# Row buffers kept for all batches, 24 or 25 scatter marks a batch, and later folds on VectorE

## The chip, the core and the metric

The kernel runs on one core of a Trainium2 chip. The metric is the device time of one execution in microseconds (us). The engines are TensorE (PE; its weight loads are shown as PEld), VectorE (DVE), ScalarE (ACT), GpSimd (POOL) and SyncE (SP, which here only issues DMA transfers). Each works through its own instructions in order and waits on semaphores for the others.

## The reference, cut to what matters

```python
def reference(x, moe..., moe2...):
    X = np.fft.fft(x, axis=1)              # x: 8 x 3072 x 256
    X = np.fft.fft(X, axis=2).real
    t = X.reshape(24576, 256)
    # group stage: each token goes to one of 8 experts
    logits = norm(t) @ norm(expert_emb).T / tau
    e = argmax(logits); gate = softmax(logits)[e]
    t = gate * (relu(t @ w1[e]) @ w2[e])   # 256 -> 1024 -> 256
    # gated stage, the same weights for all tokens
    return ((t @ w_a) * (t @ w_b)) @ w_out # 256 -> 1536 -> 256
```

The change lies in the first part: the two transforms, the choice of the expert, and the scatter of each token's row to its expert's region in DRAM.

## The kernel before

The transforms run over 8 batches b of 3072 points of time. The input of a batch comes in four chunks of 96x8x256 (`load_x`, three buffers). `fold_u` and `fold_v` make sums and differences of mirrored columns; a chunk has two halves of each, 96x508 elements. Folds of batch b+1 are made during batch b: `folds` puts them into queues, and `drain` takes some out at fixed places of the loops. In the kernel before, the `fold_v` of chunks 0 and 1 are whole (96x1016) and go to GpSimd through `fold_q`; all others go to VectorE through `dve_q`. Behind the folds of a chunk stands `rest`, which copies two columns on ScalarE and issues the load of the chunk three later.

A batch has two phases. **s1** has 16 groups of four matmuls (line 356), each copied to yt by ScalarE (360). **s2** has 12 steps t: two pairs of matmuls into psb and psa (377), the copy zs of psb on ScalarE (378), and zc from both on VectorE (382, two instructions). **s3** follows two steps behind s2: matmuls (395, 398) and on ScalarE the copy qs (406), and then VectorE writes two rows of tokens into xo (407, 409), 24 rows of 128 tokens a batch. The s3 steps 10 and 11 stand in the next batch, behind its first two s1 groups. `post` queues ScalarE's mirrored copies (421) and squares (416) of xo.

`route` chooses the experts of a batch: a chain of some 35 small VectorE instructions, advanced one at a time between the others, five groups of seven in s1 and the rest in s2 of the next batch. Its last one (557) makes the row positions, and only then are 24 scatters put into `pool_q`. They are indirect DMAs issued by GpSimd (164), one for each row of 128 tokens. `mark` takes one out of the queue (two when over 24 wait) behind certain ScalarE copies, and the scatter waits for that copy, so that the scatters are spread. In the kernel before, the marks are all 16 copies of s1 (of batches from 2 on) and the 12 of s2.

There are two xo buffers, for even and odd batches. In the kernel before, each batch takes a new tile from its pool; a new tile's first write waits until every use of the old tile in that memory is over. The odd buffer is also the setup's scratch space (`spare`).

In the last batch the group stage is prepared: `weigh` (756, 757) and `turn` of the first group of tokens stand in s2 at steps 6 and 8. When the transforms are over, their right-hand pools are freed, and the remaining scatters of batch 6 are issued without marks. The group stage splits its expert weights into two parts with a ScalarE cast (746) and a VectorE subtraction (747); one of these tiles lies where the even xo buffer was. After the group stage comes the gated stage, by far the longest part.

The named places of the order are these: step t means the t-th turn of the s2 loop, a turn the time from a batch's first zs copy to the next batch's.

Of the kernel before, what the change touches and what calls it, by code (L numbers as in the profile page):

```python
# [8 lines left out]
F32 = mybir.dt.float32  # L9
# [14 lines left out]
NT = 12  # L24
SEG = 67
ROW = 4 * SEG - 1
# [111 lines left out]
def moe_kernel(ctx, tc, x, emb, tau, w1, w2, wa, wb, wo, pa, pt, pr, nat, out):  # L138
    nc = tc.nc
    ve, sc, gp, pe, sy = nc.vector, nc.scalar, nc.gpsimd, nc.tensor, nc.sync  # L140
# [37 lines left out]
    def mark(i):  # L178

        marks[:] = [i.ins]  # L180
        drain(pool_q, 2 if len(pool_q) > 24 else 1)

    def scatter(idx_ap, src):
        i = spread(idx_ap, src, xs, NROWS - 1, "xs")
        if marks:
# [11 lines left out]
    xo_p = [p1b.enter_context(tc.tile_pool(name="xo0", bufs=1, side="right")),  # L197
            p1.enter_context(tc.tile_pool(name="xo1", bufs=1, side="left"))]
# [26 lines left out]
    def bank():  # L225
        uses[0] += 1
        return banks[uses[0] % 2][:, 0:384]

    def corner():
        uses[1] += 1  # L230
        return banks[uses[1] % 2][:, 384:512]
# [4 lines left out]
    def load_x(n):  # L236
        b, c = divmod(n, 4)
        if b == B:
            return
        t = xr_p.tile([96, 8, D], F32, name="xr")  # L240
        sy.dma_start(t, x[b].rearrange("(p n) d -> p n d", p=96)[:, 8 * c:8 * c + 8, :])
        xr[b, c] = t

    def pair(b, c):
        if (b, c) not in xf:
            xf[b, c] = big[(4 * b + c) % 6][0:96, :].rearrange("p (n d) -> p n d", n=8)
        return xr[b, c], xf[b, c]

    def fold_u(b, c, h):
        a, f = pair(b, c)  # L250
        n = slice(4 * h, 4 * h + 4)
        ve.tensor_tensor(f[:, n, 1:128], a[:, n, 1:128], a[:, n, 255:128:-1], ALU.add)

    def fold_v(b, c, eng, h):
        a, f = pair(b, c)
        n = slice(4 * h, 4 * h + 4) if h is not None else slice(0, 8)
        eng.tensor_tensor(f[:, n, 129:256], a[:, n, 1:128], a[:, n, 255:128:-1], ALU.subtract)

    def fold_e(b, c):
        a, f = xr.pop((b, c)), xf[b, c]  # L260
        sc.copy(f[:, :, 0:256:128], a[:, :, 0:256:128])
# [18 lines left out]
        return y  # L280


    spare = xo_p[1].tile([128, 2 * NT, ROW + 1], F32, name="xo").rearrange("p j c -> p (j c)")
    pcs = spare[:, 0:640]
    embt = spare[0:8, 640:896]
    su = ExitStack()
# [9 lines left out]
    ps = corner()  # L296
# [48 lines left out]
    xo = {}  # L345
    ssq = {}

    def s1(b, s):
        f = xf[b, s // 2]
        state["step"] += 1  # L350
        if s == 0:
            yts[b] = [yt_p.tile([128, NQ, 128], F32, name=f"yt{h}") for h in range(2)]
        for h in range(2):
            ps = bank()
            for n in range(4):
                pe.matmul(ps[:, 96 * n:96 * n + 96], lhsT=f[:, 4 * (s % 2) + n, 128 * h:128 * h + 128],
                          rhs=f1[0:96, :], start=True, stop=True)
            dst = yts[b][h][:, :, 16 * s:16 * s + 16].rearrange("p q (n c) -> p q n c", c=4)
            src = ps.rearrange("p (n q c) -> p q n c", n=4, c=4)
            i = sc.copy(dst, src)  # L360
            if b > 1:
                mark(i)
            elif b:
                marks[:] = [i.ins]
            if b:
                drain(act_q, 1)
# [19 lines left out]
    def s3(b, t):  # L386
        za, zb = zt.pop((b, t))
        if t == 0:
            xo[b] = xo_p[b % 2].tile([128, 2 * NT, ROW + 1], F32, name="xo")
            ssq[b] = r_p.tile([128, 2, NT], F32, name="ss", bufs=2)  # L390
        o = xo[b]
        ps = ps3.tile([128, 3, 137], F32, name="ps3")
        for i in range(2):
            q = 2 * t + i
            pe.matmul(ps[64 * i:64 * i + 64, 1, :], lhsT=tq(q), rhs=zb[:, i, :], start=True, stop=True)
        for i in range(2):
            q = 2 * t + i
            pe.matmul(ps[64 * i:64 * i + 64, 0, :], lhsT=tp(q), rhs=za[:, i, :], start=True, stop=True)
        pi = 0
        if t == 11:  # L400
            pi = 2
            for i in range(2):
                pe.matmul(ps[64 * i:64 * i + 64, 2, :], lhsT=tp2 if i else tp(22), rhs=za[:, i, :],
                          start=True, stop=True)
        qs = z_p.tile([128, 137], F32, name="qs")
        sc.copy(qs, ps[:, 1, :])
        ve.tensor_tensor(o[:, t, MAIN:MAIN + NCOL], ps[:, 0, :], qs, ALU.subtract)
        advance()
        ve.tensor_tensor(o[:, NT + t, MAIN:MAIN + NCOL], ps[:, pi, :], qs, ALU.add)
        advance()  # L410
# [15 lines left out]
        if t1 == NT:  # L426
            act_q.append(lambda: square(b, 1, 11))

    act_q, dve_q, pool_q, fold_q, routes = [], [], [], [], []

    def drain(q, n):
        for _ in range(min(n, len(q))):
            q.pop(0)()

    def folds(b):
        for c in range(4):
            dve_q.append(lambda c=c: fold_u(b, c, 0))
            dve_q.append(lambda c=c: fold_u(b, c, 1))
            if c < 2:
                fold_q.append(lambda c=c: fold_v(b, c, gp, None))  # L440
            else:
                dve_q.append(lambda c=c: fold_v(b, c, ve, 0))
                dve_q.append(lambda c=c: fold_v(b, c, ve, 1))

            def rest(c=c):
                fold_e(b, c)
                load_x(4 * b + c + 3)

            dve_q.append(lambda c=c, rest=rest: act_q.insert(0, rest))

    seg = {}
    for n in sorted({2 * (t1 - t0) for c in CHUNKS.values() for t0, t1 in c} | {2 * NT}):
        s = c1.tile([128, E, n], F32, name=f"seg{n}")
# [114 lines left out]
    def advance(n=1):  # L568
        for _ in range(n):
            if routes:  # L570
                for g in list(routes):
                    r = next(g, 0)
                    if r == 0:
                        routes.remove(g)
                    if r != 1:
                        break

    def start_route(b, t0, t1):
        routes.append(route(b, t0, t1, state["next"]))
        state["next"] += 1  # L580
# [368 lines left out]
    def first(c):  # L949
        for h in range(2):  # L950
            fold_u(0, c, h)
        fold_v(0, c, gp if c != 2 else ve, None)

    for b in range(B):
        last = b == B - 1
        if not last:
            folds(b + 1)
        for s in range(8):
            if b == 0 and s < 6:
                if s == 0:  # L960
                    routes.append(embed())
                if s % 2 == 0:
                    first(s // 2 + 1)
                else:
                    fold_e(0, s // 2 + 1)
                    load_x(s // 2 + 4)
            s1(b, s)
            if b or s > 5:
                drain(fold_q, 1)
            if b == 0:  # L970
                advance(7)
                drain(dve_q, s > 3)
                continue
            if s == 0:
                s3(b - 1, 10)
                s3(b - 1, 11)
                post(b - 1, 9, 12)
                act_q.append(lambda b=b - 1, c=CHUNKS.get(b - 1, ((0, NT),))[-1]: start_route(b, *c))
            if last:
                drain(act_q, s < 3)  # L980
                advance(8)
                if s == 0:
                    assert "tab1" in half
                    load_w(0)
                if s == 4:
                    load_w(1)
                if s in (4, 5):
                    split_w(0, s - 4)
            elif s < 3:
                drain(dve_q, 3 if s else 2)  # L990
                drain(act_q, s)
            else:
                advance(7)
        if b == 0:
            while routes:
                advance()
            su.close()
        chunks = {t1 + 1: (t0, t1) for t0, t1 in CHUNKS.get(b, ())}
        if last:
            for g in range(2):  # L1000
                load_g(g)
        for t in range(NT + (2 if last else 0)):
            if t < NT:
                s2(b, t)
            if t >= 2:
                s3(b, t - 2)
            if t in (5, 8, 11):
                post(b, t - 5, t - 2)
            if t == NT + 1:
                break  # L1010
            if t - 1 in chunks:
                act_q.append(lambda b=b, c=chunks[t - 1]: start_route(b, *c))
            if t % 3:
                drain(dve_q, 1)
            drain(act_q, 2)
            if last:
                advance(1)
                if t == 6:
                    weigh(0)
                if t == 8:  # L1020
                    turn(0)
        drain(dve_q, 20)
# [236 lines left out]
    for st in range(NST):  # L1259
        G, p = divmod(st, NP)  # L1260
# [60 lines left out]
```

## Time and profile before

| | |
|---|---|
| median of 3 runs | 3882.5 us (3882.05 to 3883.97) |
| profiled execution, its own time | 3879.51 us |
| its span, first to last instruction | 3877.7 us |
| mean granted TensorE clock | 0.985 of full |
| TensorE busy | 3773.7 us (97%) |
| VectorE busy | 3121.0 us (80%) |
| ScalarE busy | 1702.1 us (44%) |
| GpSimd busy | 1136.6 us (29%) |
| transforms, to the first group-stage matmul | about 381 us of the span |

Busy shares are means over stages with different limits. The change touches the first tenth of the program, so the rows below come from that stretch, with times counted from the start of the span. A row's bracket tells how long the engine was idle ahead of it and what released it.

### The profile page before, as it was taken

The page shows a single profiled execution, that of the slowest core. Times are in us where ns is not written, and L with a number is a line of the kernel's source. Part 1 is how long each engine was busy: PE and PEld are TensorE (multiplying, and loading weights), DVE is VectorE, ACT ScalarE, POOL GpSimd, SP SyncE. Part 2 cuts the span into 40 slices and gives each one's busy share as a digit, 9 for nine tenths or more (in the row PEclk, how much of TensorE's full clock was granted, in tenths as well). Part 3 has the DMA queues.
Part 4 walks back from the last instruction along what each step waited for, and adds up shares of the span by engine and source line. Part 5 has one row for each costly group of instructions (what it writes and reads, how often), then busy time and mean ns, then how long its engine had stood idle before and what let it go on. Part 6 is the DMA issues. An engine that isn't in the chain of part 4 may idle for free.

```text
span 3877.7 us, 68085 instructions
## 1 busy us (share of the span) xinstructions
PE 3773.7 (97%) x25556; PEld 3445.0 (89%) x25556; DVE 3121.0 (80%) x5097; ACT 1702.1 (44%) x3025; POOL 1136.6 (29%) x1017
## 2 busy tenths in 40 slices
PE   9888899999999999999999999999999999999998
PEld 8777899999999999888888888888888888888887
DVE  6766889899989987777788877788777788777886
ACT  4555566666666666433333333333333333333332
POOL 2666566667676643000000000000000000011011
PEclk8889899999999999999999999999999999999999
DMA  5444354333243231334334434444344344344331
GB/s 147 137 136 147 109 169 139 119 120 116 80 122 118 74 98 51 123 136 142 139 136 144 138 137 145 147 138 144 136 139 143 136 141 141 136 141 145 137 134 56
DMA packets 255048, 497.84 MB, mean 128 GB/s; under 512 B 151541, under 2 KB 184061, under 8 KB 245885
## 3 DMA queue, kind: packets, MB, share of 16 engines
q1 hardware_dynamic: 236284, 442.04, 35.1%
q0 software_dynamic: 18432, 51.44, 3.7%
q8 instruction: 201, 3.29, 0.3%
q14 instruction: 131, 1.07, 0.1%
HBM read 568.14 MB, written 95.14 MB: 171 GB/s over the span
## 4 chain that ended last, share of the span: by engine, by line
PE 59%; issue 18%; DVE 11%; POOL 2%; ACT 1%; DMA 0%; SPq 0%; POOLq 0%; ACTq 0%; DVEq 0%
PE pp L1142 7%; PE pp L1144 6%; PE pp L1143 6%; PE psy L819 5%; PE psy L820 5%; PE psy L821 5%; PE psh L794 5%; PE psh L790 5%; PE psh L792 4%; PE po L1212 3%; PE po L1210 3%; PE po L1211 3%; DVE big L1183 2%; DVE big L1168 2%; DVE gl L1194 1%
## 5 line engine op out<-in xcount | busy, mean ns | idle before, releaser
L164 POOL DMA_INDIRECT out_dram<-o,ig x192 | 215.3, 1121 | 2080.2 <-ACT o L1216 2033.5
L1189 ACT CAST gh<-big 128x512 fp32r<-128x512 f32 x576 | 355.8, 622 | 778.0 <-DVE big L1183 778.0
L1212 PE MATMUL po<-wo,gl 128*128 128x256 f32 x2304 | 651.1, 283 | 0.2 <-DVE gl L1194 0.2
L1210 PE MATMUL po<-wo,gh 128*128 128x256 f32 x2304 | 649.2, 282 | 1.6 <-ACT gh L1189 1.6
L1211 PE MATMUL po<-wo,gh 128*128 128x256 f32 x2304 | 647.4, 281 | 0.0
L747 DVE TENSOR_TENSOR s<-big,s 128x1024 fp32r<-128x1024 f32 x412 | 559.2, 1358 | 63.6 <-ACT s L746 62.2
L1142 PE MATMUL pp<-xo,slab 128*128 128x512 f32 x1440 | 582.8, 405 | 12.7 <-DVE big L1168 12.1
L1144 PE MATMUL pp<-xo,slab 128*128 128x512 f32 x1440 | 569.9, 396 | 0.0
L1143 PE MATMUL pp<-xo,slab 128*128 128x512 f32 x1440 | 566.7, 394 | 0.2 <-DVE xo L1126 0.2
L1211 PEld LDWEIGHTS po<-wo,gh 128*128 128x128 f32 x2304 | 435.5, 189 | 89.4
L1210 PEld LDWEIGHTS po<-wo,gh 128*128 128x128 f32 x2304 | 433.7, 188 | 88.9 <-ACT gh L1189 1.8
L819 PE MATMUL psy<-hh,s 128*128 128x256 f32 x1648 | 468.7, 284 | 13.5 <-ACT hh L802 13.5
L820 PE MATMUL psy<-hl,s 128*128 128x256 f32 x1648 | 468.4, 284 | 0.5 <-DVE hl L803 0.5
L821 PE MATMUL psy<-hh,s 128*128 128x256 f32 x1648 | 467.9, 284 | 0.0
L790 PE MATMUL psh<-xh,s 128*128 128x256 f32 x1648 | 452.9, 283 | 1.3 <-ACT xh L773 1.2
L794 PE MATMUL psh<-xh,s 128*128 128x256 f32 x1648 | 452.3, 283 | 0.0
L746 ACT CAST s<-big 128x1024 fp32r<-128x1024 f32 x412 | 428.8, 1041 | 16.4 <-DMA xs<-xo,posi 16.4
L1212 PEld LDWEIGHTS po<-wo,gl 128*128 128x128 f32 x2304 | 434.9, 189 | 0.4 <-DVE gl L1194 0.4
L1160 ACT COPY big<-pp 128x512 f32<-128x512 f32 x288 | 169.0, 587 | 584.7 <-PE pp L1144 581.9
L802 ACT ACTIVATE hh<-psh 128x512 fp32r<-128x512 f32 x412 | 246.4, 598 | 402.0 <-PE psh L794 271.1
L1194 DVE TENSOR_TENSOR gl<-big,gh 128x512 fp32r<-128x512 f32 x576 | 393.2, 683 | 2.9 <-ACT gh L1189 0.7
L1162 DVE TENSOR_TENSOR big<-pp,big 128x512 f32<-128x512 f32 x288 | 198.2, 688 | 238.2 <-PE pp L1144 209.5
(200 smaller groups left out, 8608.5 us busy)
## 6 DMA issues: line engine op xcount, KB each, us to landing
slab<-slabs SPq DMA_DIRECT2D x282, 896.0 KB
big<-in_w_dram SPq DMA_DIRECT2D x206, 1024.0 KB
big<-xs SPq DMA_DIRECT2D x103, 264.0 KB
ytd<-big SPq DMA_DIRECT2D x103, 256.0 KB
xr<-in_x_dram SPq DMA_DIRECT2D x32, 768.0 KB
big<-ytd SPq DMA_DIRECT2D x24, 1024.0 KB
slabs<-slab SPq DMA_DIRECT2D x12, 896.0 KB
xs<-xo,posi POOLq DMA_INDIRECT x192, 3.2
```

What stands on the lines that cost most here:

```text
L747: ve.tensor_tensor(lo, r, hi.bitcast(F32), ALU.subtract)
L790: pe.matmul(ps[:, i, :], lhsT=wh, rhs=hi[:, k, :], start=(k == 0 and (u > 0 or i == 0)), stop=False, skip_group_check=True)
L794: pe.matmul(ps[:, i, :], lhsT=wl, rhs=hi[:, k, :], start=False, stop=last_, skip_group_check=True)
L819: pe.matmul(ps[:, c, :], lhsT=wh, rhs=a[:, i, :], start=st, stop=False, skip_group_check=True)
L820: pe.matmul(ps[:, c, :], lhsT=wh, rhs=l[:, i, :], start=False, stop=False, skip_group_check=True)
L821: pe.matmul(ps[:, c, :], lhsT=wl, rhs=a[:, i, :], start=False, stop=(f == 7), skip_group_check=True)
L1142: pe.matmul(ps, lhsT=t[:, wh, :], rhs=xh, start=start, stop=False, skip_group_check=True)
L1143: pe.matmul(ps, lhsT=t[:, wh, :], rhs=xl, start=False, stop=False, skip_group_check=True)
L1144: pe.matmul(ps, lhsT=t[:, wl, :], rhs=xh, start=False, stop=True, skip_group_check=True)
L1210: pe.matmul(ps, lhsT=ht, rhs=wos[0][:, f, :], start=(first_ and r % 2 == 0), stop=False, skip_group_check=True)
L1211: pe.matmul(ps, lhsT=ht, rhs=wos[1][:, f, :], start=False, stop=False, skip_group_check=True)
L1212: pe.matmul(ps, lhsT=lt, rhs=wos[0][:, f, :], start=False, stop=last_, skip_group_check=True)
```

## The change

One xo tile for each parity is made at the start and used by all batches, so that the order of accesses is kept for each row and no longer for a whole tile. All `fold_v` of batches from 1 on go to VectorE in halves, `fold_q` is gone, and each of the 12 steps of s2 now takes one entry out of `dve_q` (before: two steps of three). In s1 only the second copy of each pair marks a scatter (from batch 2 on), and in s3 the copy qs of every third step does so too.

```diff
-    spare = xo_p[1].tile([128, 2 * NT, ROW + 1], F32, name="xo").rearrange("p j c -> p (j c)")
+    xos = [p.tile([128, 2 * NT, ROW + 1], F32, name="xo") for p in xo_p]
+    spare = xos[1].rearrange("p j c -> p (j c)")
...
             i = sc.copy(dst, src)
-            if b > 1:
+            if b > 1 and h:
                 mark(i)
-            elif b:
+            elif b == 1:
                 marks[:] = [i.ins]
...
         if t == 0:
-            xo[b] = xo_p[b % 2].tile([128, 2 * NT, ROW + 1], F32, name="xo")
+            xo[b] = xos[b % 2]
...
-        sc.copy(qs, ps[:, 1, :])
+        i = sc.copy(qs, ps[:, 1, :])
+        if b and t % 3 == 2:
+            mark(i)
...
-            if c < 2:
-                fold_q.append(lambda c=c: fold_v(b, c, gp, None))
-            else:
-                dve_q.append(lambda c=c: fold_v(b, c, ve, 0))
-                dve_q.append(lambda c=c: fold_v(b, c, ve, 1))
+            dve_q.append(lambda c=c: fold_v(b, c, ve, 0))
+            dve_q.append(lambda c=c: fold_v(b, c, ve, 1))
...
             s1(b, s)
-            if b or s > 5:
-                drain(fold_q, 1)
...
-            if t % 3:
-                drain(dve_q, 1)
+            drain(dve_q, 1)
```

Two of its effects on the order of the instructions are on VectorE. Here is the start of s2 in batch 2 before, from step 1 to the zc of step 3; line 382 is zc, 257 a fold of v, the others belong to the route. The names behind "waits" are semaphores, DMASW0 to 7 those of the scatters' transfers.

```order
L382 SCALAR_TENSOR_TENSOR zc<-sgnx,psb,psa 128x137
L521 TENSOR_REDUCE mx<-ex 128x24
L257 TENSOR_TENSOR big_71<-xr 96x4x127 [waits Pool_49]
L382 SCALAR_TENSOR_TENSOR zc<-sgnx,psb,psa 128x137 [waits PE_49,Activation_49]
L524 TENSOR_TENSOR acc<-acc,inc 128x8 [waits DVE_49]
L382 SCALAR_TENSOR_TENSOR zc<-sgnx,psb,psa 128x137
L535 TENSOR_SCALAR mx<-mx 128x24 [waits DVE_49]
L407 TENSOR_TENSOR xo<-ps_1303,qs 128x137 [waits DMASW4_49,DMASW3_49,DMASW5_49,DMASW2_49,DMASW6_49,DMASW1_49,DMASW7_49,DMASW0_49,Activation_49]
L538 COPY xo<-natt 128x24
L409 TENSOR_TENSOR xo<-ps_1303,qs 128x137
L540 RECIPROCAL mx<-mx 128x24 [waits DVE_49]
L257 TENSOR_TENSOR big_71<-xr 96x4x127
```

The same stretch now, from the end of step 0 on (zc is line 383, the writes into xo are 410 and 412):

```order
L257 TENSOR_TENSOR big_70<-xr 96x4x127
L383 SCALAR_TENSOR_TENSOR zc<-sgnx,psb,psa 128x137 [waits PE_49,Activation_49]
L514 SCALAR_TENSOR_TENSOR inc<-seg_182,oh 128x192 [waits DVE_49]
L383 SCALAR_TENSOR_TENSOR zc<-sgnx,psb,psa 128x137
L521 TENSOR_REDUCE mx<-ex 128x24
L383 SCALAR_TENSOR_TENSOR zc<-sgnx,psb,psa 128x137 [waits PE_49,Activation_49]
L524 TENSOR_TENSOR acc<-acc,inc 128x8 [waits DVE_49]
L383 SCALAR_TENSOR_TENSOR zc<-sgnx,psb,psa 128x137
L535 TENSOR_SCALAR mx<-mx 128x24 [waits DVE_49]
L410 TENSOR_TENSOR xo<-ps_1298,qs 128x137 [waits DMASW0_49,Activation_49]
L538 COPY xo<-natt 128x24
L412 TENSOR_TENSOR xo<-ps_1298,qs 128x137 [waits DMASW1_49]
```

The first write into xo waited for all eight semaphores of the scatters, and now each write waits for one, that of its own row; a fold that stood in step 1 stands in step 0, and further folds follow in steps 2 to 5 and 7 to 10.

On GpSimd this is the order from the last folds of the transforms to the first group's copy (757) and weighing (756), before:

```order
L164 DMA xs<-xo,posi 198912x267 x22
L257 TENSOR_TENSOR big_73<-xr 96x8x127
L164 DMA xs<-xo,posi 198912x267 x2
L257 TENSOR_TENSOR big_74<-xr 96x8x127
L164 DMA xs<-xo,posi 198912x267 x43
L757 COPY big_69<-big_69 32x8
L164 DMA xs<-xo,posi 198912x267 x18
L756 TENSOR_TENSOR big_70<-big_69 128x512
```

And now, from the setup's last instructions on:

```order
L460 MEMSET padt 128x2
L257 ISA
L257 TENSOR_TENSOR big_70<-xr 96x8x127
L257 TENSOR_TENSOR big_72<-xr 96x8x127
L164 DMA xs<-xo,posi 198912x267 x147
L757 COPY big_69<-big_69 32x8
L164 DMA xs<-xo,posi 198912x267 x21
L756 TENSOR_TENSOR big_70<-big_69 128x512
```

Behind the two folds of batch 0 stand scatters alone, and three of them have moved from before the copy of line 757 to behind it.

## Rows read from the trace of the kernel before

**Rows 1.** The page: granted TensorE clock, 40 equal slices of the span.
```profile
PEclk8889899999999999999999999999999999999999
```

**Rows 2.** Stretches from each batch's first zs copy; busy us and instructions by engine.
```profile
core 0: us, PE busy (x) PEld busy (x) DVE busy (x) ACT busy (x) POOL busy (x), PEclk, DMA share, GB/s
...
79.63:116.56 36.93, 36.16 (x328) 32.20 (x327) 32.27 (x100) 24.89 (x82) 20.59 (x18) 1.00 0.49 138
116.56:163.55 46.99, 38.66 (x330) 34.14 (x329) 32.83 (x101) 24.99 (x82) 29.54 (x27) 0.89 0.47 138
163.55:210.93 47.38, 39.02 (x330) 34.52 (x329) 32.83 (x101) 25.05 (x81) 29.54 (x27) 0.89 0.46 138
210.93:258.50 47.57, 39.24 (x330) 34.73 (x329) 32.85 (x101) 25.06 (x81) 29.55 (x27) 0.89 0.46 135
258.50:307.14 48.64, 40.41 (x336) 35.26 (x335) 33.80 (x122) 25.05 (x81) 30.50 (x27) 0.89 0.45 137
307.14:355.77 48.63, 40.36 (x334) 35.43 (x333) 32.05 (x133) 26.76 (x83) 28.09 (x30) 0.89 0.44 151
```

**Rows 3.** Waits, 40 to 560 us: total, times, longest.
```profile
DVE xo L407 <- DMA xs<-xo,posi: 48.2, 6, 8.9
```

**Rows 4.** Timeline of VectorE, batch 4: start, us, instruction, idle before it.
```profile
224.08 0.30 DVE L407 TENSOR_TENSOR xo<-ps,qs 128x137 f32<-128x137 f32 x1 [8.74 <-DMA xs<-xo,posi]
...
224.38 0.29 DVE L409 TENSOR_TENSOR xo<-ps,qs 128x137 f32<-128x137 f32 x1
```

**Rows 5.** Timeline of TensorE, batches 4 and 7.
```profile
224.82 0.72 PE L395 MATMUL ps<-zs,tpq 128*64 128x137 f32 x4 [7.13 <-DVE xo L409]
...
365.36 0.46 PE L395 MATMUL ps<-zs,tpq 128*64 128x137 f32 x4 [2.54 <-DVE xo L409]
```

**Rows 6.** Timeline of GpSimd, batch 4.
```profile
197.38 2.37 POOL L257 TENSOR_TENSOR big<-xr 96x1016 f32<-96x1016 f32 x1
199.91 1.26 POOL L164 DMA_INDIRECT xs<-xo,posi  x1 [0.17 <-ACT yt L360]
201.48 1.47 POOL L164 DMA_INDIRECT xs<-xo,posi  x1 [0.31 <-ACT big L261]
...
221.52 0.97 POOL L164 DMA_INDIRECT xs<-xo,posi  x1 [0.30 <-issue]
```

**Rows 7.** Timeline of VectorE, two narrow windows: folds of batch 4's s1.
```profile
197.32 2.98 DVE L252 TENSOR_TENSOR big<-xr 96x508 f32<-96x508 f32 x1
...
200.23 1.87 DVE L252 TENSOR_TENSOR big<-xr 96x508 f32<-96x508 f32 x3
```

**Rows 8.** Timeline of VectorE, batch 1, steps 4 to 6 of s2.
```profile
87.59 0.35 DVE L382 SCALAR_TENSOR_TENSOR zc<-sgnx,psb,psa 128x137 f32<-128x137 f32 x1
...
88.36 0.62 DVE L382 SCALAR_TENSOR_TENSOR zc<-sgnx,psb,psa 128x137 f32<-128x137 f32 x2
...
89.98 0.64 DVE L382 SCALAR_TENSOR_TENSOR zc<-sgnx,psb,psa 128x137 f32<-128x137 f32 x2
```

**Rows 9.** Timeline of TensorE there: the psb matmuls of steps 6 and 7.
```profile
88.31 0.74 PE L377 MATMUL psb<-rhb,yt 128*128 128x138 f32 x4
...
90.07 0.74 PE L377 MATMUL psb<-rhb,yt 128*128 128x138 f32 x4
```

**Rows 10.** Timeline of GpSimd, end of the transforms.
```profile
369.71 0.97 POOL L164 DMA_INDIRECT xs<-xo,posi  x1 [1.27 <-ACT zs L378]
...
374.69 0.99 POOL L164 DMA_INDIRECT xs<-xo,posi  x1 [0.63 <-ACT zs L378]
...
397.39 0.97 POOL L164 DMA_INDIRECT xs<-xo,posi  x1 [0.31 <-DMA xs<-xo,posi]
```

**Rows 11.** Timeline of ScalarE, start of the group stage.
```profile
400.03 1.04 ACT L746 CAST s<-big 128x1024 fp32r<-128x1024 f32 x1 [16.37 <-DMA xs<-xo,posi]
```

**Rows 12.** Timeline of TensorE there.
```profile
402.01 0.58 PE L819 MATMUL psy<-hh,s 128*128 128x256 f32 x1 [13.49 <-ACT hh L802]
```

**Rows 13.** Stretches at the start of the group stage, columns as in rows 2.
```profile
402.00:412.00 10.00, 9.24 (x38) 8.36 (x39) 9.95 (x15) 7.33 (x12) 4.09 (x3) 0.50 0.00 0
412.00:422.00 10.00, 10.00 (x85) 10.00 (x85) 8.23 (x20) 7.19 (x15) 2.97 (x2) 1.00 0.21 55
```

More of the change, by code (lines that the diff above doesn't have):

```diff
@@ L427, in post @@
             act_q.append(lambda: square(b, 1, 11))
-    act_q, dve_q, pool_q, fold_q, routes = [], [], [], [], []
+    act_q, dve_q, pool_q, routes = [], [], [], []
     def drain(q, n):
```

## The prediction

> **What bounds the kernel now.** The page comes first. TensorE is busy nearly throughout, so time is gained where it waits or runs slowly; the clock row shows 8 in place of 9 in slices 1 to 3 and 5 of 40, early in the program, where the transforms stand [rows 1]. Next I read the table of stretches, cut at the first zs copy (line 378) of each batch, so that a stretch is one turn from batch to batch. Batch 1 takes 36.93 us, with TensorE busy 36.16 of them at full clock. Batches 2 to 6 take 46.99 to 48.64 us with hardly more TensorE work and a mean granted clock of 0.89 [rows 2]. So a turn can be done in 37 us and takes 47 in five batches; I look for what ends these 10 us.
>
> The list of waits names it: VectorE's line 407, the first write into xo, waits for the row scatters six times, 48.2 us in all [rows 3]. In the timeline of batch 4 it starts at 224.08 after 8.74 us of waiting [rows 4], line 409 behind it ends at 224.67 (224.38 and 0.29), TensorE's next s3 matmul starts at 224.82 after 7.13 [rows 5], and the last scatter of the batch two before was issued at 221.52 [rows 6]. It is a whole-tile wait: a new xo tile takes the memory of the old one, and its first write waits for all 24 scatters of that old tile (first order fence). The clock is granted in two levels, full or half, so a mean of 0.89 says that part of each such turn runs at half: its 10 us are 7 of waiting and 3 of slow matmuls.
>
> The scatters end late because GpSimd is full: each takes 0.97 us plus 0.30 to the next, 24 of them 30.5 us, and between them stand two folds of 2.37 us [rows 6]. They can start only when the routing of that batch has made its positions, in step 4 of the next s2.
>
> **The change part by part.** *Kept tiles.* With one tile per parity for all batches, the write of step t waits for its own two rows' scatters alone (second fence). Which one comes closest? Row 23 of batch k-2 is scattered at the mark of s2 step 4 of batch k and rewritten by s3 step 11, seven steps and two s1 groups later: over 12 us at 1.75 us a step [rows 9]. From issue to release the last scatter of rows 6 took 2.6 us (221.52 to 224.08). Behind a late write stand the next zc and so TensorE, but with some 9 us of margin the new waits cost nothing. What ends a turn then is what ends it in batch 1, where no tile is awaited: TensorE itself. Gain, against 36.93: 10.06, 10.45 and 10.64 in batches 2 to 4 [rows 2]. Batches 5 and 6 are longer by 1.07 and 1.06 than batch 4, with more instructions on TensorE and VectorE (the tables, the routing in two halves), which stays; so 10.64 each. Sum 52.4. Batch 7 has a shorter wait of the same kind, 2.54 us on TensorE [rows 5]: 2.5.
>
> *Folds on VectorE.* Four folds of 96x508 replace two on GpSimd in each of the turns from batch 1 to batch 6. Alone, such a fold costs 0.62 us (three in 1.87); beside a GpSimd fold the same instruction took 2.98 [rows 7]. So VectorE pays for the GpSimd folds already: it loses 2 x 2.4 and gets 4 x 0.6 instead. That gain is in s1, where VectorE then waits for ScalarE's squares before it can route, so I count it as nothing. What can cost is the other side: s2 has nine folds instead of six. In s2 VectorE runs without a gap until step 5 [rows 8]. In the kernel before it has two folds behind it at step 4 (of steps 1 and 2), now three (of steps 0, 2 and 3). The second zc of step 4 ends at 87.94 and TensorE's psb matmul that needs its buffer starts at 88.31 [rows 8, 9]. One fold more makes it 88.54, and a release takes 0.15 (224.67 to 224.82 in rows 4 and 5), so TensorE is late by 0.38. From step 5 on a step with a fold is 1.62 us of VectorE (88.36 to 89.98) [rows 8] against 1.75 of TensorE [rows 9], and VectorE catches up. The bounds: nothing, or all three extra folds on the path, 1.8. I take 0.38, six times: minus 2.3 (bounds 0 and 10.8).
>
> The four input loads of a turn are issued behind the folds: one at the same place, one a step after s1 instead of within it, one at step 6 instead of 4, one at step 11 as before. Each is used nine or more steps later, some 16 us. A turn moves the same bytes; batch 1 moved 138 GB/s in 36.93 us with the DMA engines half busy [rows 2], and by that rate a 768 KB load takes an estimated 5.6 us. Cost nothing; without that cover a late load costs its lateness once a turn.
>
> *Marks.* A turn has 8 marks in s1, 12 in s2 and 4 in s3, so a scatter each 1.55 us of a 37.3 us turn; GpSimd needs 1.28. So it keeps up, and the queue ends at the same distance from the transforms' end, with one exception. In batch 7 the first GpSimd copy of the group stage (line 757) waits for all scatters before it; it stands behind the scatter of s2 step 6 in both kernels, but now 21 scatters follow it and not 18 (the two GpSimd fences). In the kernel before the scatter of step 6 started at 369.71, the first behind the copy at 374.69 and the last at 397.39 [rows 10]. Three more at 1.28 us end 3.8 us later. ScalarE's cast into memory of the old xo tile waits for the last one (16.37 us) [rows 11], and TensorE for that cast (13.49 us) [rows 12]. So this is on the path: minus 3.8. Bounds: nothing, if another wait ends there, and twice that. The longer idle time may also stretch the half clock that follows it: 10 us at 0.50 did 38 matmul records, the next 10 us at full clock 85 [rows 13]. Another such stretch would cost 5.5 us; I take a seventh, minus 0.8.
>
> *Sum.* 52.4 + 2.5 - 2.3 - 3.8 - 0.8 = 48.0 us. The profiled execution took 3879.5 us (span 3877.7), which gives 3831.5. The median of the runs, 3882.5, lies 3.0 above it, so I predict 3834.5. The stages behind are TensorE-bound and move forward as they are.
>
> **Rivals.** First, *scatters stretched by folds*. The scatters beside VectorE folds took 1.26 and 1.47 us, not 0.97 [rows 6]. If all 24 were stretched to 1.47, with 0.30 between, GpSimd would need 42.5 us a turn, 5.2 more than the turn. The backlog passes the margin of the row waits after two or three turns; then three or four turns last 42.5 (some 16 us), and what is left of the backlog, some 16, ends in the last wait: 48 - 32 = 16, 3866. Against it: in a turn 16 folds fill 10 us of 37, so about a quarter of the scatters meets one, and there is 0.27 to spare for each of the 24. [...]
>
> Second, *VectorE binds more than I count*: the extra folds cost their full 1.8 us, and the tail is dearer: 48.0 - 8.6 - 5 = 34, 3848. For it: no gap in steps 0 to 5 [rows 8]. Against: the folds of steps 7 to 10 lie where it has gaps.
>
> Third, *slower*: the contention the other way, in s2. If a running scatter held up a fold as the GpSimd fold does (2.98 in place of 0.62, though only for a scatter's 0.97), each of 16 folds would cost 1.0 more, 16 us a turn; VectorE's 30 us (32.8 less 4.8 plus 2.5) would become 46, and with the s2 chain the turn about 48, in batch 1 and without a gain in the others, and the longer tail on top: plus 11 and 4, 3897. It decides from 0.5 us per fold (48 us over 96 folds). Against it: three folds in 1.87 us [rows 7] while scatters ran at 199.91 and 201.48 [rows 6].
>
> Fourth, *no change*: something else holds the first s3 write as long, a late load for instance. The list of waits shows no load for that stretch.
>
> **How the numbers follow.** Forecast 72% (own range 3826 to 3843: the bounds on the folds, the tail and its clock, and 0 to 3 us more gain if the tail does not lengthen or batch 7's start gets shorter). VectorE binds 12%, scatters stretched 7%, no change 3%, slower 6%. A measurement here tells 0.2% (about 8 us) from no change: faster 0.91, same 0.03, slower 0.06. The range reaches up to the second rival: 3826 to 3850.
>
> **What would show it.** In the profile after: turns of 37 to 38.5 us at full clock for batches 1 to 6; no VectorE wait for row scatters in the transforms; no clock dip between the first batch and the group stage; GpSimd with gaps before each scatter that ScalarE's marks end; the first cast of the group stage waiting about 20 us in place of 16. Wrong would be: turns over 40 us, TensorE waiting for zc in s2 for more than 1 us a turn, back-to-back scatters into the next turn, or row waits at step 11.

## The result, and the profile after

The changed kernel takes 3841.7 us (median of four runs, 3835.8 to 3845.5) against 3883.2 us before on the same chip: ratio 0.9894, 95% interval [0.9882, 0.9907]. The gain is 41.6 us where 48.0 were forecast, and the time lies inside the forecast's range. The profiled execution took 3843.6 us (span 3841.4, 36.3 less than before). In the experiments below, three single runs (4533.7, 11506.6 and 6074.2 us, of after2, mend and oldmarks) had mean clocks of 0.748, 0.308 and 0.553, where the other runs of these kernels have 0.979 to 0.993, and all times and ratios leave them out.

The turns, cut as in [rows 2] (us, then busy us and instructions of TensorE, its weight loads, VectorE, ScalarE and GpSimd, granted clock, DMA share, GB/s), batch 1 first:

```profile
81.20:119.20 38.00, 36.39 (x328) 32.25 (x328) 29.80 (x104) 24.98 (x82) 20.69 (x19) 1.00 0.54 149
119.20:157.30 38.10, 36.50 (x330) 32.35 (x329) 29.99 (x104) 24.98 (x81) 26.65 (x25) 1.00 0.59 170
157.30:195.50 38.20, 36.60 (x330) 32.46 (x330) 29.98 (x104) 25.01 (x81) 26.75 (x25) 1.00 0.59 170
195.50:233.70 38.20, 36.60 (x330) 32.45 (x329) 29.98 (x104) 25.05 (x82) 26.75 (x25) 1.00 0.60 170
233.70:273.10 39.40, 37.56 (x336) 32.73 (x335) 31.38 (x124) 24.96 (x81) 24.29 (x24) 1.00 0.65 188
273.10:317.60 44.50, 42.83 (x334) 38.64 (x334) 34.07 (x140) 26.98 (x84) 26.99 (x26) 0.87 0.48 160
```

Batches 2 to 5 are 8.9 to 9.4 us shorter, at full clock. Batch 1 is 1.1 longer, and batch 6 gained only 4.1: its clock is 0.87. VectorE's wait for row scatters [rows 3] is gone; its list of waits between 40 and 345 us has no such line.

Three places cost more than I had counted. First, TensorE in batch 3 (start, us, instruction, idle before it and what ended it):

```profile
158.80 0.71 PE L378 MATMUL psb<-rhb,yt 128*128 128x138 f32 x4 [0.56 <-DVE zc L383]
...
160.48 0.39 PE L530 MATMUL ps<-inc,prt 128*128 128x8 f32 x2 [0.51 <-DVE inc L514]
...
186.77 7.39 PE L357 MATMUL ps<-f,big 96*128 96x96 f32 x64 [0.46 <-ACT yt L361]
```

The wait for zc is not new; in batch 2 before it was 0.70 us:

```profile
118.16 0.71 PE L377 MATMUL psb<-rhb,yt 128*128 128x138 f32 x4 [0.70 <-DVE zc L382]
```

What is new is 0.51 us for the routing's scan `inc` and 0.46 us for a yt copy in s1. VectorE around the first, and ScalarE around the second:

```profile
158.57 0.62 DVE L510 TENSOR_TENSOR oh<-t,mt 128x192 f32<-128x192 f32 x1
158.96 0.73 DVE L257 TENSOR_TENSOR big<-xr 96x508 f32<-96x508 f32 x1
159.61 0.35 DVE L383 SCALAR_TENSOR_TENSOR zc<-sgnx,psb,psa 128x137 f32<-128x137 f32 x1
159.88 0.55 DVE L514 TENSOR_TENSOR_SCAN inc<-seg,oh 128x192 f32<-128x192 f32 x1
```

```profile
184.56 0.48 ACT L361 COPY yt<-ps 128x384 f32<-128x384 f32 x1
185.06 0.29 ACT L426 COPY xo<-xo 1x128 f32<-1x128 f32 x1
185.37 0.52 ACT L424 COPY xo<-xo 128x384 f32<-128x384 f32 x1
185.92 0.29 ACT L426 COPY xo<-xo 1x128 f32<-1x128 f32 x1
186.24 0.48 ACT L361 COPY yt<-ps 128x384 f32<-128x384 f32 x1
```

A fold now stands between `oh` and `inc`, and the small matmul that needs `inc` stands in TensorE's queue ahead of the next s3. In s1 three xo copies stand between two yt copies.

Second, the tail, over 325 to 425 us (total, times, longest), against 16.37 and 13.49 before [rows 11, 12]:

```profile
ACT s L746 <- DMA xs<-xo,posi: 20.2, 1, 20.2
...
PE psy L819 <- ACT hh L802: 17.2, 1, 17.2
```

Third, batch 7's s1 ran at half clock (granted 0.50) from 305.7 to 319.3 us. TensorE is busy for all of its 13.60 us; ahead of it, it had waited only 0.25 and 0.33 us:

```profile
305.70:319.30 13.60, 13.60 (x65) 13.60 (x64) 8.33 (x35) 5.19 (x11) 4.62 (x5) 0.50 0.50 151
```

```profile
302.63 2.02 PE L357 MATMUL ps<-f,big 96*128 96x96 f32 x16 [0.25 <-ACT yt L361]
...
305.36 10.29 PE L357 MATMUL ps<-f,big 96*128 96x96 f32 x48 [0.33 <-DVE pref L547]
```

GpSimd keeps up, but not as forecast. I had expected a gap before each scatter; of the 139 scatters in these six turns only 40 start after more than the 0.30 us that lie between two in any case, and the others follow one another. At the end of s1 they wait for their marks again, so that no backlog passes on. Scatters beside VectorE's folds took up to 1.49 us instead of 0.97 (batch 3):

```profile
163.13 1.12 POOL L164 DMA_INDIRECT xs<-xo,posi  x1 [1.23 <-ACT zs L379]
...
173.17 1.40 POOL L164 DMA_INDIRECT xs<-xo,posi  x1 [0.31 <-issue]
174.87 1.44 POOL L164 DMA_INDIRECT xs<-xo,posi  x1 [0.30 <-ACT junk L419]
...
191.38 0.97 POOL L164 DMA_INDIRECT xs<-xo,posi  x1 [0.80 <-ACT yt L361]
```

### The profile page after: what moved, and what is told of

Read it like the earlier page. It is cut to its first block, busy times and chain, and to the rows that moved or that the text cites. A ratio compares the mean times of both kernels' runs of the same rounds, so it can differ in the third digit from the quotient of the medians.

```text
span 3841.4 us, 68162 instructions
## 1 busy us (share of the span) xinstructions
PE 3768.5 (98%) x25556; PEld 3440.0 (90%) x25556; DVE 3109.2 (81%) x5125; ACT 1702.8 (44%) x3025; POOL 1113.1 (29%) x1003
## 4 chain that ended last, share of the span: by engine, by line
PE 76%; DVE 17%; issue 3%; POOL 2%; ACT 1%; DMA 1%; SPq 0%; POOLq 0%; ACTq 0%; DVEq 0%
PE pp L1139 9%; PE pp L1141 9%; PE pp L1140 9%; PE po L1209 5%; PE po L1207 5%; PE po L1208 5%; PE psy L819 5%; PE psy L820 5%; PE psy L821 5%; PE psh L794 4%; PE psh L790 4%; PE psh L792 3%; DVE big L1180 3%; PE ps L357 2%; DVE big L1165 2%
## 5 line engine op out<-in xcount | busy, mean ns | idle before, releaser
L819 PE MATMUL psy<-hh,s 128*128 128x256 f32 x1648 | 467.6, 284 | 17.2 <-ACT hh L802 17.2
```

The costliest lines, as they stand in the source:

```text
L819: pe.matmul(ps[:, c, :], lhsT=wh, rhs=a[:, i, :], start=st, stop=False, skip_group_check=True)
```

## The experiments

They ran on four chips, on which the kernel before takes 3877.8 us (chip 3), 3881.8 (chip 11), 3892.2 (chip 0) and 3907.3 (chip 5); ratios are to before on the same chip. The record gives no number for the chip of the result's own runs; it is called the first below.

**First set, chip 0: the parts one by one.** tiles, the kept buffers alone:

```diff
-    spare = xo_p[1].tile([128, 2 * NT, ROW + 1], F32, name="xo").rearrange("p j c -> p (j c)")
+    xos = [p.tile([128, 2 * NT, ROW + 1], F32, name="xo") for p in xo_p]
+    spare = xos[1].rearrange("p j c -> p (j c)")
...
-            xo[b] = xo_p[b % 2].tile([128, 2 * NT, ROW + 1], F32, name="xo")
+            xo[b] = xos[b % 2]
```

> The kernel before with the kept row buffers alone; its folds on GpSimd and its marks stay. Theory (the row waits were the whole gain, the rest of the change only costs): the turns of batches 2 to 6 fall from 47.0 to 48.6 us to about 37.3 (38.4 in batches 5 and 6), no VectorE wait for row scatters is left in the transforms, the first cast of the group stage still waits about 16.4 us, and the time is 3828 to 3834, below the changed kernel's 3841.7. Rival (the change needs its folds on VectorE, because GpSimd is too full): 24 scatters of 1.28 us and two folds of 2.4 us, lengthened by VectorE's, fill 36 to 40 us of a turn, a backlog builds up, VectorE waits for rows again at steps 8 to 11, turns are 39 to 41 and the time is 3850 to 3865.

folds, the folds on VectorE alone:

```diff
-            if c < 2:
-                fold_q.append(lambda c=c: fold_v(b, c, gp, None))
-            else:
-                dve_q.append(lambda c=c: fold_v(b, c, ve, 0))
-                dve_q.append(lambda c=c: fold_v(b, c, ve, 1))
+            dve_q.append(lambda c=c: fold_v(b, c, ve, 0))
+            dve_q.append(lambda c=c: fold_v(b, c, ve, 1))
...
-            if t % 3:
-                drain(dve_q, 1)
+            drain(dve_q, 1)
```

> The kernel before with all folds of later batches on VectorE alone; row buffers are taken anew as before, marks as before. Theory (the stall ended when a full GpSimd had done its last scatter): two GpSimd folds of 2.4 us leave the path, each of the five stalls of about 7 us shrinks by 4 to 5, six turns pay 1.2 for VectorE, and the time is 3862 to 3870. Rival (the stall's end is set by ScalarE's marks and by when the positions are there, not by GpSimd's work): the stalls stay at 7 us, the time is 3885 to 3892.

oldmarks, the changed kernel with the marks of before:

```diff
-            if b > 1 and h:
+            if b > 1:
                 mark(i)
-            elif b == 1:
+            elif b:
                 marks[:] = [i.ins]
...
-        i = sc.copy(qs, ps[:, 1, :])
-        if b and t % 3 == 2:
-            mark(i)
+        sc.copy(qs, ps[:, 1, :])
```

> The changed kernel with the old marks (both copies of each step of s1, none in s3). Theory (the marks matter only at the tail): turns stay at 38.2 us, 18 scatters instead of 21 follow the copy that waits, the first cast waits 16.4 us instead of 20.2, time 3836 to 3839. Rival (denser marks in s1 put scatters back to back beside the folds, which then take longer and hold up VectorE and TensorE): turns of 38.7 us or more, time 3841 to 3846.

poolfolds is the changed kernel with the diff of folds taken back.

> The changed kernel with the folds as before (two of 96x1016 a batch on GpSimd, VectorE folds at two of three steps of s2); kept buffers and the new marks stay. Theory (the 1.2 us that a turn lost against 36.93 come from VectorE's extra folds in s2): TensorE's wait for inc (0.5 us a turn) goes, turns are 37.3 to 37.6, time 3835 to 3838 with the tail as in the changed kernel. Rival (GpSimd cannot do 24 scatters and two folds in a turn with 24 marks): backlog, row waits come back, GpSimd has no gaps, time 3850 or more.

Measured: tiles 3892.2 (0.9998 [0.9984, 1.0011]), folds 3890.2 (0.9991 [0.9978, 1.0004]), oldmarks 3895.1 (1.0004 [0.9990, 1.0018]), poolfolds 3877.6 (0.9958 [0.9941, 0.9975]). Every theory missed; folds and poolfolds have the times of their rivals. But the stalls were not those of the rivals: ScalarE waited for TensorE's semaphores long after the recorded matmuls, in folds and oldmarks at the end of s1, in tiles and poolfolds mostly at the start of s2. The rows of the third set show it.

**Second set, chip 11: before and after again, marks alone, and a mended tail.**

> The changed kernel again, unchanged, beside the others of this set. Theory (all three parts are needed together: kept buffers, folds off GpSimd and sparser marks in s1): the time stays 1.0 to 1.1% below the kernel before on the same chip, turns of 38.2 us, no TensorE result that comes late. Rival (the chip of the last set was slower at TensorE by itself, and any kernel there shows results of TensorE's matmuls that come 2 to 5 us late in s1): the gain is below 0.4% and the late results show here too.

> The kernel before again, unchanged, for a profile on the same chip as the others. Theory (the kernel decides): the picture of the first profile, VectorE waiting for row scatters in s2, TensorE's results never late, turns of 47 to 48.6 us, ratio 1.000. Rival (the chip decides): turns as long, but the stall stands in the end of s1, with results of TensorE that come 2 to 5 us after the matmul, as in the kernels with old marks of the last set.

marks is the kernel before with the diff of oldmarks taken the other way.

> The kernel before with the new marks alone; row buffers and folds as before. Theory (marks alone only spread the scatters and cannot end the wait for the whole old buffer): 24 marks instead of 28 a turn let the last scatter start later, stalls as long or up to 2 us longer a turn, tail 3.8 us longer, 3884 to 3900 where before is 3883. Rival (the marks are what gains, by sparser scatters in s1): at least half of the changed kernel's gain, 20 us or more.

mend, against the changed kernel:

```diff
-            if b > 1 and h:
+            if b > 1 and (h or b == B - 1):
...
-    slots[1] = [[sl1_p.tile([128, 2048], F32R, name=f"s1{w}{i}") for i in range(2)] for w in range(2)]
+    slots[1] = [[sl1_p.tile([128, 2048], F32R, name=f"s1{w}{i}") for i in range(2)] for w in (1, 0)][::-1]
```

> The changed kernel with the tail mended in two ways: batch 7's s1 has marks on both copies, so 13 scatters instead of 21 follow the copy that waits for rows; and the two weight buffers that lie in the old row buffer are those that are cast two steps later. Theory (the tail's wait of 20.2 us on ScalarE is on the path and ends with the last of these scatters): 8 scatters at 1.28 us less and two steps of some 2.9 us of work ahead of the wait take 14 to 17 us off it, 3824 to 3832 where the changed kernel is 3841.7. Rival (TensorE then waits for something else, the late weights or the half clock): a gain of 5 us or less.

after2 took 3841.0 us (0.9896 [0.9881, 0.9911]) and before2 3881.1 (0.9999 [0.9990, 1.0008]), with the pictures of the first chip and no late semaphores. Whether the chip or the kernel makes late semaphores, the set cannot tell: no profile of either kernel was taken on chip 0, where the changed kernel did not run at all. That all three parts are needed falls with tiles3 below. In the profile of after2, its fastest run (3837.0), the half clock of batch 7's s1 is missing, with the same work there and the same two waits ahead of it (0.24 and 0.33 us):

```profile
271.80:311.30 39.50, 37.66 (x334) 33.09 (x334) 32.89 (x135) 26.82 (x83) 26.55 (x26) 1.00 0.51 175
```

That is 5.0 us less than the row 273.10:317.60 above. So this dip does not come in every run of the kernel.

marks alone gained, against my theory and less than its rival: 3873.7 (0.9980 [0.9971, 0.9989]). The stalls stay but are shorter (VectorE's waits in marks, then in before2, 116 to 420 us):

```profile
DVE xo L409 <- DMA xs<-xo,posi: 36.5, 6, 8.3
```

```profile
DVE xo L407 <- DMA xs<-xo,posi: 47.4, 6, 8.8
```

Turns of batches 2 to 6 are 3.3 to 3.7 us shorter than in before2. Batch 7 loses 6.5 of that (27.2 us from its first to its last zs copy instead of 20.7, a full stall), and TensorE's tail wait is 16.1 instead of 13.5. The new marks allow three more scatters in s2 and seven fewer in s1. The traces show what that does: in s2 of batch 3 GpSimd waits for marks for 1.3 us and in before2 for 6.2 (GpSimd's waits over that turn, in marks, then in before2), and the last scatter of each of these batches starts some 7.4 us after the next turn's first zs copy instead of some 10.5.

```profile
POOL xs L164 <- ACT zs L378: 1.3, 2, 1.0
```

```profile
POOL xs L164 <- ACT zs L378: 6.2, 8, 1.5
```

So GpSimd was not full in the kernel before, though I had written that it was (the sum does not use it); a part of the stall came from the marks. No further run tested this.

mend beats both kernels: 3829.5 (0.9867 [0.9849, 0.9885]), 11.5 us below after2 and inside the expected 3824 to 3832, though the wait did not shrink by the expected 14 to 17 us. TensorE's wait in the tail, in after2 and in mend (the second view is a timeline):

```profile
PE psy L819 <- ACT hh L802: 14.8, 1, 14.8
```

```profile
353.44 0.58 PE L790 MATMUL psh<-xh,s 128*128 128x256 f32 x1 [10.53 <-ACT xh L773]
```

The wait is 4.3 us shorter than in after2 and is another one. ScalarE's cast still waits for the rows (11.1 us), but that is no longer what TensorE waits for; it waits for xh, made from a product (line 756) that stands behind the 13 scatters in GpSimd's queue. The cast of xh also stands behind the waiting cast in ScalarE's queue. The half clock after it lasts 10.2 us instead of 17.1, but TensorE is busy in it for 3.4 us and in after2 for 3.9, so this explains little. The two profiles differ by 7.5 us (spans 3827.3 and 3834.8); what else makes these up, and which of mend's two edits did how much, no run shows.

**Third set, chip 5: tiles, oldmarks and poolfolds again.**

> The kernel with the kept row buffers alone, once more. In its first run, on another chip, semaphores of TensorE came up to 4 us after the last recorded matmul, which no run of the kernel before or of the changed kernel shows. Theory (that was the chip): without it the five stalls go, turns of batches 2 to 6 are 37 to 39 us, the first cast waits about 16 us, time 3828 to 3840 where before is 3882. Rival (that was the kernel: kept buffers with old marks and folds on GpSimd always end so): turns of 44 to 56 us, late semaphores again, the time within 0.2% of before.

> The changed kernel with the old marks, once more. Theory (the first run was disturbed by its chip; the marks matter only at the tail): turns of 38.2 us, tail 3 to 4 us shorter than the changed kernel's, time 3835 to 3841 where the changed kernel is 3842. Rival (two scatters a step in s1 hold up TensorE's semaphores whatever the chip): turns of 47 us with the stall at the end of s1, time within 0.3% of before.

> The changed kernel with the old folds (two a batch on GpSimd), once more. Theory (VectorE's extra folds cost about 1 us a turn, and GpSimd can do both): turns of 37.0 to 37.6 us, TensorE's wait for inc gone, time 3835 to 3840. Rival (24 scatters at 1.28 us and two folds do not fit into a turn of 37 us with 24 marks): GpSimd without gaps, its backlog grows by 2 us or more a turn, row waits come back in batch 5 or 6, turns of 39 to 43 us there, time 3850 to 3870.

tiles2 3908.0 (1.0003 [0.9994, 1.0012]), oldmarks2 3899.0 (0.9976 [0.9966, 0.9985]), poolfolds2 3890.4 (0.9953 [0.9939, 0.9967]). tiles2 and oldmarks2 came out as their rivals say; poolfolds2 has a time above both its ranges. The turns (42 to 55 us in poolfolds2) and the late semaphores are like those of the first set. oldmarks2, ScalarE and then TensorE at the end of batch 3's s1:

```profile
163.99 0.48 ACT L361 COPY yt<-ps 128x384 f32<-128x384 f32 x1 [0.56 <-PE ps L357]
166.95 0.48 ACT L361 COPY yt<-ps 128x384 f32<-128x384 f32 x1 [2.49 <-PE ps L357]
171.96 0.48 ACT L361 COPY yt<-ps 128x384 f32<-128x384 f32 x1 [4.53 <-remote]
```

```profile
160.74 4.92 PE L357 MATMUL ps<-f,big 96*128 96x96 f32 x42
167.49 1.13 PE L357 MATMUL ps<-f,big 96*128 96x96 f32 x8 [1.83 <-issue]
172.50 2.02 PE L357 MATMUL ps<-f,big 96*128 96x96 f32 x8 [3.88 <-issue]
```

The copy at 171.96 needs only matmuls that are recorded before 165.7. Neither engine has other work; TensorE's semaphore updates stand in the trace at 166.93 and 171.94, the second some 6.3 us behind the matmuls that the copy needs. The traces of these two chips hold 25,822 to 26,079 semaphore updates, those of the others 30,047 to 30,126. In the last 2200 us, where all kernels are instruction for instruction the same, it is 12,276 to 12,444 against 14,353 to 14,363. So this goes with the chip and not with the kernel, if one kernel shows both. The last run shows it:

> The kernel with the kept row buffers alone, a third time, for a chip that does not lose semaphore updates: in the two sets where TensorE's results came late, the traces hold some 26,000 updates in place of 30,050, and the updates are missing in the last stage too, where the kernels do not differ, so the late results belong to those chips. Theory (the row waits are nearly the whole gain): on a chip with 30,000 updates the five stalls go, turns of batches 2 to 6 are 37 to 39 us, 3828 to 3840 where before is 3882, as fast as the changed kernel or faster. Rival (without fewer marks or without folds off GpSimd the scatters of a batch are not done in a turn): row waits at the late steps of s2 or GpSimd without gaps, turns of 40 us or more, 3850 to 3875. If updates are missing again, 44 to 56 us a turn and a time within 0.2% of before.

tiles3, chip 3: 30,126 updates, none late, and **3827.7 us, 0.9871 [0.9854, 0.9887]**. So the late semaphores go with the chip. The theory holds, at the lower end of its 3828 to 3840 us, and VectorE has no wait for row scatters between 40 and 345 us (batches 2 to 6):

```profile
117.40:154.70 37.30, 36.39 (x331) 32.42 (x330) 32.61 (x101) 25.03 (x82) 29.62 (x27) 1.00 0.60 174
154.70:192.00 37.30, 36.39 (x331) 32.42 (x330) 32.60 (x101) 25.05 (x82) 29.63 (x27) 1.00 0.61 173
192.00:229.30 37.30, 36.39 (x331) 32.42 (x330) 32.57 (x101) 25.03 (x82) 29.61 (x27) 1.00 0.61 175
229.30:267.60 38.30, 37.41 (x336) 32.77 (x335) 33.28 (x122) 25.03 (x82) 30.67 (x27) 1.00 0.57 173
267.60:306.40 38.80, 37.46 (x334) 33.08 (x333) 31.52 (x133) 26.73 (x82) 28.62 (x30) 1.00 0.57 193
```

GpSimd is nearly full and keeps up, with the folds between the scatters:

```profile
214.72 0.97 POOL L164 DMA_INDIRECT xs<-xo,posi  x1 [0.30 <-ACT qs L407]
215.71 2.36 POOL L257 TENSOR_TENSOR big<-xr 96x1016 f32<-96x1016 f32 x1
218.23 1.26 POOL L164 DMA_INDIRECT xs<-xo,posi  x1 [0.17 <-ACT yt L361]
```

Its tail is that of before (16.4 and 13.5 us), and its four runs lie within 0.9 us. The kept buffers alone thus seem faster than the whole change; by ratio the rest of it costs 0.25% (0.9896 less 0.9871), some 9.7 us. The two ratios are from different chips and their intervals just overlap; the profiles say the same with 8.3 us (spans 3834.8 and 3826.5). tiles3 ties with mend. The kept buffers with a mended tail were not run.

## Why the prediction was right, and where its sizes were off

| Term | Forecast | Measured |
|---|---|---|
| Stalls of batches 2 to 6 | +52.4 | +50.2 (tiles3 against [rows 2]: 9.7, 10.1, 10.3, 10.3, 9.8) |
| Stall of batch 7 | +2.5 | +2.6 (21.5 before, 18.9 in tiles3, from first to last zs copy) |
| Folds on VectorE | -2.3 | -5.4 (turns of after2 less those of tiles3: 1.0, 0.8, 0.9, 0.9, 1.1, 0.7) |
| Tail | -3.8 | -3.7 in the first profile (17.2 less 13.5), -1.3 in after2 |
| Longer half clock after the tail | -0.8 | 0 in length: 20.5 us in before and after; TensorE was busy in it for 9.2 us before and 5.2 after |
| Half clock in batch 7's s1 | none | -5.0 in the first profile, 0 in after2 |

Measured, that is 38.7 for the first profile (span 36.3 shorter; 1.6 of the rest is a later first batch, 81.20 instead of 79.63) and 46.1 for after2 (46.4 shorter than before2). The terms come from several chips, so that the sums agree this well is in part luck. So is it that the time lies below 3843, the end of the forecast's own narrower range: the half clock ahead of batch 7 was not in it, and the two slower of the four runs (3843.6 and 3845.5) are beyond.

*Kept tiles.* Right, and shown alone by tiles3: the whole-tile wait was the stall, nothing else took its place, and the row waits cost nothing. The size is 2 us too large because I took batch 1 as the measure. From batch 2 on the routing has two more small matmuls, those of line 533 here, 0.37 us, which batch 1 lacks (rows of tiles3, 154.7 to 192.0; the counts x328 and x330 in [rows 2] show them):

```profile
L531 PE MATMUL ps<-inc,prt 128*128 128x8 f32 x2 | 0.4, 266 | 0.0
L533 PE MATMUL ps<-acc,ones 128*128 128x8 f32 x2 | 0.4, 256 | 0.0
```

*Folds on VectorE.* The step that failed, inside its bounds (0 to 10.8). "One fold more makes it 88.54 ... TensorE is late by 0.38" put the cost on zc's buffer. That late start did not come, and TensorE's waits for zc did not grow (TensorE's waits from 43 to 345 us, in tiles3 and in after2):

```profile
PE psb L378 <- DVE zc L383: 5.0, 7, 1.1
...
PE ps L357 <- ACT yt L361: 0.2, 1, 0.2
```

```profile
PE psb L378 <- DVE zc L383: 4.5, 7, 1.1
PE ps L530 <- DVE inc L514: 3.1, 6, 0.5
PE ps L357 <- ACT yt L361: 3.0, 7, 0.5
```

Two others came: `inc` behind the extra fold, 3.1 us, and yt, 2.8 more; with 0.5 less for zc that is the 5.4 by which the turns differ. after2 has the new marks besides the moved folds. Where no row buffer is awaited, in batch 1, the marks alone change nothing (36.94 us in marks, 36.93 in before2, 37.95 in after2), so I put the loss down to the folds; folds alone never ran on a chip without late semaphores. The second came by ScalarE: the small copies (line 261) that follow the folds of a chunk had stood between the xo copies in s1 and now stand elsewhere, so that three xo copies meet. I had followed what moved on VectorE and not what it moved on ScalarE. That link is read from the timelines of after and tiles3; it was not tested by itself.

*Tail.* The three more scatters were there in both profiles, but the wait grew by 3.7 us in the first and by 1.3 in after2. From the first scatter behind the copy of line 757 to the last took 22.7 us before, 26.4 in the first profile and 25.6 in after2; before and in the first profile one of them was stretched to 1.9 and 1.8 us, in after2 none. And these scatters start when that copy has waited for the scatter ahead of it, 4.0 us ahead of the last zs copy in after2, 2.4 in the first profile and 2.6 before. The copy in the first profile, then in after2:

```profile
332.84 0.19 POOL L757 COPY big<-big 32x8 int32<-32x8 int32 x1 [3.47 <-issue]
```

```profile
325.33 0.19 POOL L757 COPY big<-big 32x8 int32<-32x8 int32 x1 [1.79 <-DMA xs<-xo,posi]
```

So the price of a scatter was right, and the sum left out that the start of the row moves; why it moved is open.

*Clock.* That a mean of 0.89 is a part of the turn at half clock shows in batch 4 before: granted 1.00 from 216.84 to 220.80 us, 0.50 to 231.10 and 1.00 to 241.00. I forecast no dip ahead of the group stage. after2 and tiles3 have none; the first profile has one of 13.7 us. The four runs of that chip had mean clocks of 0.992, 0.991, 0.989 and 0.988 with spans of 3833.7, 3837.6, 3841.4 and 3843.3 us: the lower the clock, the longer the span of these four. TensorE's waits ahead of the dip do not differ between the two profiles. Why it falls in some runs of this kernel, and hardly varies in tiles3, stays open.

*Rivals.* "Scatters stretched by folds" did not come true, though more scatters met a fold than the quarter that I had counted: 81 of the 139 in the six turns, which took 1.18 us on average and the others 0.97. That is some 3 us a turn, and GpSimd still waits for marks at the end of s1. "VectorE binds more" named the right engine and was right in half: 5.4 us, not 10.8. "Slower" had nothing: the recorded folds of these turns took 0.62 to 0.73 us. "No change" had nothing where the changed kernel ran; on the chips with late semaphores the kept buffers alone changed nothing, for another reason than the one I gave.

## What to carry to other kernels

A wait for a whole reused buffer can be removed by keeping the buffer and letting each row wait for its own use; do that alone first, since the two edits that came with it here seem to have cost 8 to 10 of its 50 us. When work moves to an engine with room, look at each small instruction that a third engine waits for (here `inc`) and at what the moved work issues on other engines (here ScalarE's small copies), not at the busy share. Take as the measure of a clean turn one that does all of the work: batch 1 lacked two matmuls.

## What the runs showed of the hardware

The same kernel, with the kept buffers alone, gains 1.3% on one chip and nothing on two others. There TensorE's semaphore updates came late in the transforms (by some 6.3 us in the rows of oldmarks2 above), and a seventh of all updates is missing from the trace (26,006 and 25,822 in tiles and tiles2, 30,126 in tiles3). No run shows what makes them late, or why a part of them is missing. Open are also what the changed kernel does on such a chip, which was not run there, and what folds alone do on one without late semaphores.

Beside VectorE's folds of 96x508 elements a scatter held GpSimd for up to 1.49 us, and for 0.97 to 1.08 without one (the six turns of the first profile). The clock fell to half for 13.6 us in one run of a kernel behind waits of 0.25 and 0.33 us, and in another run behind waits of 0.24 and 0.33 us it did not.
